# Output stores of a fused attention, Fourier-mixing and FFN kernel as a stream of steps of their own, rows of 514 elements, and a new order of the steps

## The chip, the cores and the metric

One core of one Trainium2 chip. The metric is the device time of one execution in microseconds (us), less is better. A core has five engines that work through queues of their own: TensorE (PE, with its weight loads shown as PEld), VectorE (DVE), ScalarE (ACT), GpSimd (POOL) and SyncE (SP), and DMA queues that SP, ACT and POOL issue to.

## The reference

For 8 batches of 8 heads, 576 rows and 64 columns, linear attention with a feature map, then Fourier mixing, a normalisation and an FFN:

```python
def phi(x):                                   # x: 8 x 8 x 576 x 64, w_phi: 64 x 128
    proj = np.einsum('bhsd,df->bhsf', x, w_phi)
    proj = proj - np.max(np.abs(proj), axis=-1, keepdims=True)
    return np.concatenate([np.exp(proj), np.exp(-proj)], axis=-1)
kv  = np.einsum('bhsf,bhsd->bhfd', phi(k), v)
z   = np.sum(phi(k), axis=2)
num = np.einsum('bhsf,bhfd->bhsd', phi(q), kv)
den = np.einsum('bhsf,bhf->bhs', phi(q), z)[..., None] + 1e-06
x   = (num / den)                             # heads side by side: 8 x 576 x 512
u   = x + np.real(fft(fft(x, axis=1), axis=2))
un  = (u - mean(u)) / np.sqrt(var(u) + 1e-06)
out = u + np.maximum(un @ w_ch1, 0.0) @ w_ch2 # 512 -> 2048 -> 512, fp32 out
```

## The kernel before

Every batch goes through the same stages, and stages of two or three batches run at the same time on the five engines.

**Attention.** POOL loads K, Q and V of a batch with casting DMAs (L281) into KS, QS and VS. SP turns them over by DMA transposes into KT (L411, L413) and QT (L423 to L425); for batch 0 PE does it (L371, pst) and ACT or DVE casts the result (L376, L378). PE projects K (psk, L505; batch 0: L788), ACT takes the exponentials (KPp and KPn, L511; batch 0: L794), DVE the maxima MK (L525; batch 0: L822), POOL scales V by them (V4S L444, VC L462), and PE sums kv (L844, L848). Of Q, PE makes psq (L559) for the maxima MQ (DVE, L567) and psh (L600) for the exponentials (ACT, L609). PE applies kv (pn, L969), DVE and POOL divide; POOL writes the quotient to X (L989).

**Mixing.** The rows are folded by symmetry (DVE, L862 to L886, R), multiplied by cosine and sine tables on PE (psD, L1031 and L1070; pu, L1127), and added to X (DVE, L1114). The tables SS, CS, SD and CD are made by ACT's sines at the start (L217 to L228) and doubled by DVE (L237). DVE takes the statistics (L1197), ACT writes the normalised rows UN (L1173), SP transposes them to UT (L1190).

**FFN** (`forward`, 68 steps a batch). `hidden` makes psf = W1b x UT (L1247, ACT's relu to HT L1252 or L1254) and `output(c)` makes pso (L1264) for one row block c of 128 rows; the last 64 rows are at L1290. DVE adds the scaled pso to X (L1270, L1297). Then `store(b, U, c)` issues the block's DMAs to the output, mostly on SP: four for c = 1 (L1224), one for c = 2 and c = 3 (L1230), two for c = 4 (L1233, L1234); the last half block of the last batch goes at L1320. A block of X thus holds the block of the output until it is stored, and X has three buffers.

**The order.** Nothing is scheduled by a tool at build time: every piece of work is a generator that yields between steps, and a string PLAN with one letter per step says which generator goes on next. An engine's queue is the order in which the steps issue to it; `tc.manual_schedule()` keeps it. The letters: F forward, M mixing, D folds, N normalise, U scales, P maxima of Q, T features, R maxima of K, S scaled V, K, V and Q loads, A and B the transposes of Q and K, W weight loads, G and J the first transposes on PE, C and H tables and sines, Z memsets, and Y the stirs, seven groups of four matmuls on ones whose result nobody reads (L1362). The end of `output` and the place where PLAN is read:

```python
            nc.vector.scalar_tensor_tensor(
                out=U[:, c, 0:C], in0=po[:], scalar=scale_of[b, c], in1=U[:, c, 0:C],
                op0=ALU.mult, op1=ALU.add,
            )
            store(b, U, c)
            yield
...
    with tc.manual_schedule():
        ...
        for name in PLAN:
            step(name)
```

PSUM is in three pools: pj (two buffers of two banks), pk (one) and pb (three; psf and pso among others).

Of the kernel before, what the change touches and what calls it, by code (L numbers as in the profile page):

```python
# [20 lines left out]


PLAN = (
    "CCYCCGCGZHZHCHHTZGGTHJTKHPQTTJZKRWSRJYTTRGJSSPRTYPTRJTMMYPTSTMMPSTTZPTMPTBKZTMQMMQMHTTHMMVTAMMMDYDYD"
    "TDTMRTMVTMRSMTMMMVMTRPTMTMNRMTNNTWSYMTNNMFTSPFUFMTRFMUNFFSNFFFFMNMTKNPUPPFMFMPTTTNSFPFFUUQMMMQUFFTFM"
    "FFMMFFUMFFMVFMFMFFQFBVKFKAFFTDTDTDDTFFRFFFFTFFHFFRFRFFTMTFMFRSFTFFFFFTMMFRFFSMFPTVMTFFMSTFTQNMFFFNPP"
    "MPMMMTFSMMTPFFFTSFPQTMQVMPFBFTFFNAFMMNFMFFNMFFMFMFFMFFFDFFUMFFFMFMFFTTPFFTFFTFRFDVFFTFFQFFQRKFFFDFFR"
    "FSVDTPFRKFFFMFTFTMFFMFFFVTMFFRSMFTPMFTTMNNFFMMFMQFMFFSSMTFMTFFFNFSTPPMFTFMBFPTFPAMFFFMFNTFKMMFFFNFMF"
    "MFFMFFUMQMFFVMFFFTTPFFFFMTFFRFTTFFVFFFRFFRFDFFFFDFDFFDPTFMFTTFFFFMKFRFTMSFMRFFMFTSPMFNTMPQNSFFFFQMMM"
    "MTTTFFBMSFFFFTPMTFSFFMFFMTPVMFFFFMTPNFFNNMMMFFMAFFFMUFMFKMFFFMFFTTDTTFRFFSFFFFRVFFTMFFFFFRPTFFDFFFDR"  # L30
    "FFFTDFMFVKTPFFFFFMTMBQMFFRSFMFTSTSTMMKFFFNNSFMMFMMFTFMFPTMKFFFFPTPMTFFMFFFNMFTPPMFFFTNFQMNMVFFMFQMFM"
    "FFMUFFMFFVMAFFFFTTTTFDRFRFFTFSFFFFMRFFQFFFDFFTFFFDFFRFVDFTFMFFTTMFFMFFMFRSMFQTTTMFTQFNFMSVFFMFFTNPMM"
    "FMSTPMTFFFFSMTPPMFTFFMPPFBAFMFPFMFNNFMMVFMFMFFFMTTFRMNUFFFFFMRFFFMFFFSTFFMFFPTFFTFFFDDFFFRFTFFFDFDVR"
    "FFFMFTTFFMFMTMFRFFSMFFSFMTTNTFFMFNMMFFFMMFTFMPSTFNFFFPTFMFFTMPFFFFMPSPMFFTMFFPFTMNFFFNMFMFFFUMFMFMFF"
    "FFMFFMFMFFFFFDFFDFFFFFDFFFDFMFFFMFMFFMMFFMFNFMNFFFFFFMFFFFFMNFFFMFFNFFFFFFFFFFFFFFFNUFFFFFFFFFFFFFFF"
    "FFFFFFFFFFFFFFFFFFFFFFFFFFFFFFFFFFFF"
)


# [1 line left out]
def kernel(  # L41
# [1194 lines left out]
    def forward(b):  # L1236
        U, UT = turned_u[b]
# [22 lines left out]
        def output(c):  # L1260
            at = PLACE[c]
            po = pb.tile([128, C], F32, tag="pb", name="pso")
            for hh in range(NHH):
# [6 lines left out]
            nc.vector.scalar_tensor_tensor(  # L1270
                out=U[:, c, 0:C], in0=po[:], scalar=scale_of[b, c], in1=U[:, c, 0:C],
                op0=ALU.mult, op1=ALU.add,
            )
# [156 lines left out]
```

## Time and profile before

| | us |
|---|---|
| runs | 418.07, 418.28, 424.57 |
| median | 418.28 |
| the profiled execution | 417.52 |
| its span, first to last instruction | 415.7 |

The profiled execution is one of its own, beside the three runs. 1.82 us of it lie around the span. In the profile a line such as `start us, us, engine line op out<-in xcount [idle before <-releaser]` is one instruction, or several alike in a row; the bracket is the time for which the engine stood before it, and what ended that. "SPq" and "POOLq" are the issuing of DMAs, not the transfers.

### The profile page before, as it was taken

Reading aid. Unit: us, or ns where it says so; the run is one execution under the profiler, and the core shown is the slowest. Engines: PE = TensorE matmul, PEld = TensorE weight load, DVE = VectorE, ACT = ScalarE, POOL = GpSimd, SP = SyncE. Lnnn points to the kernel's source line nnn. Section 1 sums busy time; section 2 is a strip of 40 time slices with the busy share of each in tenths; the row PEclk is TensorE's granted clock in tenths of the full one; section 3 lists DMA queues with packets and bytes.
Section 4 is the critical chain, followed back from the end, with each engine's and each line's share of the span. In section 5 each row is a group of like instructions: output and inputs, shape, how many; then the busy total and the mean of one; then the engine's idle time right before and its main releaser. Section 6 shows DMA issues by size and latency. Waiting matters only on the chain.

```text
span 415.7 us, 10465 instructions
## 1 busy us (share of the span) xinstructions
PE 391.2 (94%) x4195; PEld 265.3 (64%) x4224; DVE 317.5 (76%) x658; ACT 297.7 (72%) x548; POOL 208.1 (50%) x251
## 2 busy tenths in 40 slices
PE   4888999989999999999889999999999999999995
PEld 2556678735866568566765578566856577657564
DVE  7777887799898786898579887988889768966102
ACT  4986889778848887597858888699757886454350
POOL 4678438768746771906756382648362332301000
PEclk9899999999999999999999999999999999999998
DMA  8999798994899759663952969659882051006213
GB/s 220 195 203 146 80 187 102 135 96 88 123 161 103 96 98 152 81 99 67 139 100 40 154 118 139 91 75 101 104 125 52 18 99 33 22 7 111 36 27 88
DMA packets 108520, 42.71 MB, mean 103 GB/s; under 512 B 82615, under 2 KB 103479, under 8 KB 108471
## 3 DMA queue, kind: packets, MB, share of 16 engines
q0 software_dynamic: 46272, 16.60, 37.5%
q1 hardware_dynamic: 61703, 24.85, 33.3%
q8 instruction: 33, 0.54, 0.6%
q10 hardware_dynamic: 496, 0.59, 0.5%
q14 instruction: 16, 0.13, 0.2%
HBM read 36.77 MB, written 9.44 MB: 111 GB/s over the span
## 4 chain that ended last, share of the span: by engine, by line
PE 75%; DVE 12%; ACT 5%; POOL 3%; issue 2%; DMA 1%; POOLq 0%; DVEq 0%; ACTq 0%
PE psf L1247 27%; PE pso L1264 20%; PE pso L1290 4%; PE kv L844 4%; PE psD L1031 3%; DVE MQ L567 2%; PE pu L1127 2%; PE psk L505 2%; PE psq L559 2%; PE psh L600 1%; PE psD L1070 1%; POOL X L989 1%; DVE cb L983 1%; DVE R L862 1%; PE idle L1362 1%
## 5 line engine op out<-in xcount | busy, mean ns | idle before, releaser
L1247 PE MATMUL psf<-UT,W1b 128*128 128x320 bf16 (+1 forms) x1024 | 139.8, 286 | 1.8 <-DVE MQ L567 1.8
L1264 PE MATMUL pso<-W2b,HT 128*128 128x512 bf16 x467 | 117.2, 379 | 2.1 <-issue 1.0
L1247 PEld LDWEIGHTS <-W1b 128*128 128x128 bf16 x1024 | 95.3, 98 | 29.1 <-issue 3.8
L462 POOL TENSOR_TENSOR VC<-VS,VC 128x1024 bf16<-128x1024 bf16 x28 | 53.8, 1932 | 39.1 <-ACT VC L456 37.7
L1264 PEld LDWEIGHTS <-HT 128*128 128x128 bf16 x496 | 45.2, 98 | 43.3 <-issue 0.6
L1252 ACT ACTIVATE HT<-psf 128x320 bf16<-128x320 f32 x128 | 53.7, 437 | 25.9 <-PE psf L1247 19.0
L989 POOL TENSOR_TENSOR X<-cb,rd 128x640 f32<-128x640 f32 x28 | 35.1, 1254 | 45.9 <-DVE rd L987 25.6
L567 DVE TENSOR_REDUCE MQ<-psq 128x8 f32<-128x1024 f32 (+1 forms) x32 | 34.3, 1086 | 14.1 <-PE psq L559 13.9
L1270 DVE SCALAR_TENSOR_TENSOR X<-pso,rs,X 128x512 f32<-128x512 f32 x31 | 23.1, 744 | 28.3 <-PE pso L1264 28.1
L1254 ACT ACTIVATE HT<-psf 128x512 bf16<-128x512 f32 x64 | 37.6, 600 | 7.1 <-PE psf L1247 6.6
L525 DVE TENSOR_REDUCE MK<-psk 128x8 f32<-128x1024 f32 x28 | 33.7, 1211 | 2.9 <-ACT KPn L511 2.8
L281 POOL DMA_DIRECT2D QS<-in_q_dram x49 | 33.5, 690 | 0.9 <-issue 0.9
L609 ACT ACTIVATE QPHP<-psh 128x1024 bf16<-128x1024 f32 x28 | 28.7, 1026 | 7.2 <-PE psh L600 6.8
L511 ACT ACTIVATE KPp<-psk 128x1024 bf16<-128x1024 f32 x28 | 28.8, 1030 | 6.6 <-PE psk L505 6.3
L1173 ACT ACTIVATE UN<-X,MV 128x512 bf16<-128x512 f32 (+1 forms) x35 | 25.0, 723 | 11.8 <-DVE MV L1198 9.3
L511 ACT ACTIVATE KPn<-psk 128x1024 bf16<-128x1024 f32 x28 | 28.7, 1027 | 0.0
L609 ACT ACTIVATE QPHN<-psh 128x1024 bf16<-128x1024 f32 x28 | 28.7, 1027 | 0.0
L1197 DVE BATCH_NORM_STATS2 st<-X 128x6 f32<-128x512 f32 (+1 forms) x40 | 27.1, 678 | 0.2
L444 POOL TENSOR_TENSOR V4S<-VS,V4S 64x512 bf16<-64x512 bf16 x14 | 14.9, 1061 | 23.2 <-ACT V4S L441 21.7
L1114 DVE TENSOR_TENSOR X<-pu,X 128x512 f32<-128x512 f32 (+3 forms) x49 | 23.5, 526 | 3.7 <-PE pu L1127 3.3
L969 PEld LDWEIGHTS <-QPHP 128*128 128x128 bf16 x280 | 20.7, 98 | 7.0 <-DVE cb L983 2.8
L1213 POOL TENSOR_TENSOR rs<-VE,mhalf 128x5 f32<-128x5 f32 (+1 forms) x9 | 10.3, 1148 | 26.4 <-DVE VE L1212 26.2
(465 smaller groups left out, 771.3 us busy)
## 6 DMA issues: line engine op xcount, KB each, us to landing
out_dram<-X SPq DMA_DIRECT2D x31, 128.0 KB
out_dram<-X SPq DMA_DIRECT2D x15, 256.0 KB
KS<-in_k_dram POOLq DMA_DIRECT2D x7, 512.0 KB, 8.5
VS<-in_v_dram POOLq DMA_DIRECT2D x14, 256.0 KB, 4.9
W1b<-in_moe_w_ch_dram POOLq DMA_DIRECT2D x1, 2048.0 KB, 16.4
W2b<-in_moe_w_ch_dram POOLq DMA_DIRECT2D x1, 2048.0 KB, 16.1
QS<-in_q_dram POOLq DMA_DIRECT2D x28, 64.0 KB, 3.9
QS<-in_q_dram POOLq DMA_DIRECT2D x7, 256.0 KB, 6.0
```

The source lines that it names most:

```text
L281: nc.gpsimd.dma_start(out=pieces[i][0], in_=pieces[i][1])
L462: nc.gpsimd.tensor_tensor(out=to[:, :, :, 0:D], in0=V[:, hs, :].rearrange("p h (j d) -> p (h j) d", d=D).unsqueeze(1) .to_broadcast([128, ...
L511: nc.scalar.activation(out=KP[:, hs, :, :].rearrange("p e (jp jj) f -> p jj (e jp) f", jj=2), in_=psk[:], func=AT.Exp, scale=sgn,)
L525: nc.vector.tensor_reduce(out=MK[:, 1, 2 * pr:2 * pr + 2, :].rearrange("p e (jp jj) -> p jj (e jp)", jj=2), in_=tiles[pr][:], axis=AX.X, o ...
L567: nc.vector.tensor_reduce(out=o, in_=i[:], axis=AX.X, op=ALU.max, apply_absolute_value=True)
L609: nc.scalar.activation(out=o, in_=psh[:], func=AT.Exp, scale=sgn)
L989: nc.gpsimd.tensor_tensor(out=X[:, :, at:at + 2 * D].rearrange("p c (e d) -> p e c d", e=2), in0=cb[:, :, :, 0:D], in1=rd[:].to_broadcast( ...
L1197: nc.vector.bn_stats(out=st[0:M, :], in_=X[0:M, c, 0:C])
L1247: nc.tensor.matmul(ps, lhsT=W1b[:, cc, 128 * hh:128 * hh + 128], rhs=UT[:, cc, lo:hi], start=(cc == 0), stop=(cc == NCC - 1),)
L1252: nc.scalar.activation(out=HT[:, hh, lo:hi], in_=ps, func=AT.Relu, scale=-1.0)
L1254: nc.scalar.activation(out=HT[:, hh - 1:hh + 1, lo:hi], in_=psw[:].rearrange("p (a n) -> p a n", a=2), func=AT.Relu, scale=-1.0,)
L1264: nc.tensor.matmul(po[:], lhsT=HT[:, hh, at:at + 128], rhs=W2b[:, hh, :], start=(hh == 0), stop=(hh == NHH - 1),)
```

## The change

- `store` is no longer called from `forward`. A new generator `store_all(b)` calls it for the blocks 2, 1, 3, 4 of a batch, one a step; for the last batch 2, 1, 4, and then the two halves of block 3. It is a stream of its own, letter O, with 33 steps.
- The three places that allocate from X's pool take 514 elements a row, where they took 513. What is read and written of a row stays 512.
- PLAN is new throughout, with 1269 letters where it had 1236: the 33 O, and as many as before of every other.

```diff
 PLAN = (
-    "CCYCCGCGZHZHCHHTZGGTHJTKHPQTTJZKRWSRJYTTRGJSSPRTYPTRJTMMYPTSTMMPSTTZPTMPTBKZTMQMMQMHTTHMMVTAMMMDYDYD"
+    "CCCCCGHGHZZHZCHHYHTTGTJGRKWTQGRPTRZYSJTTJPSYRTSJTPYKRTJMMPTSTHPSMMTTPTMQPTTQVHMMMMTTMMTZMBMMYADDYDTT"
...
-        xpool.tile([128, 5, C + 1], F32, tag="X", name=n)[:].rearrange("p a b -> p (a b)")
+        xpool.tile([128, 5, C + 2], F32, tag="X", name=n)[:].rearrange("p a b -> p (a b)")
...
                 op0=ALU.mult, op1=ALU.add,
             )
-            store(b, U, c)
             yield
...
-        store(b, U, 4)
         yield
         if b < B - 1:
             return
-        rows_ = out[b, 320:576, :].rearrange("(a r j) n -> a r j n", r=32, j=2)
-        for queue, at in ((nc.scalar, 0), (nc.sync, 256)):
+        for at in (0, 256):
...
+            yield
+
+    def store_all(b):
+        U = turned_u[b][0]
+        for c in (2, 1, 3, 4) if b < B - 1 else (2, 1, 4):
+            store(b, U, c)
+            yield
+        if b < B - 1:
+            return
+        rows_ = out[b, 320:576, :].rearrange("(a r j) n -> a r j n", r=32, j=2)
+        for queue, at in ((nc.scalar, 0), (nc.sync, 256)):
             queue.dma_start(out=rows_[:, ::-1, 0, at:at + 256], in_=U[:, 3, at:at + 256])
             yield
...
-        "A": (arrive, 1), "B": (arrive_k, 1), "W": (load_ffn_weights, 2),
+        "A": (arrive, 1), "B": (arrive_k, 1), "O": (store_all, 4), "W": (load_ffn_weights, 2),
...
-    LONGER = {("N", 0): 10, ("U", 0): 7, ("M", 0): 27, ("T", 0): 20}
+    LONGER = {("N", 0): 10, ("U", 0): 7, ("M", 0): 27, ("T", 0): 20, ("O", 7): 5}
```

What the new PLAN moves shows on the engines' queues. The rows of the changed kernel carry its own line numbers: the stirs of L1362 stand at L1369 there, and L1297 at L1296.

ACT near the start, before: the casts of batch 0's turned K, the four tables, and the first exponentials of K.

```order
L383 CAST wphi_95<-wphi_f 128x128
L376 CAST KT_168<-pst 128x256
L376 CAST KT<-pst 128x512
L217 ACTIVATE SS<-gs 128x960
L221 ACTIVATE CS<-ga,halfpi 128x960
L226 ACTIVATE SD<-ga 128x512
L228 ACTIVATE CD<-ga,halfpi 128x512
L779 ACT_TABLE_LOAD
```

and with the change:

```order
L383 CAST wphi_95<-wphi_f 128x128
L376 CAST KT_168<-pst 128x256
L217 ACTIVATE SS<-gs 128x960
L376 CAST KT<-pst 128x512
L221 ACTIVATE CS<-ga,halfpi 128x960
L226 ACTIVATE SD<-ga 128x512
L228 ACTIVATE CD<-ga,halfpi 128x512
L779 ACT_TABLE_LOAD
```

The table SS has moved between the two casts. POOL at the same time, before, with the loads of batch 1 (KS and QS), the first weight load (W1b) and the scaling of batch 0's V:

```order
L281 DMA KS_271<-in_k_dram 64x8x64
L281 DMA QS_287<-in_q_dram 32x8x128 x4
L268 MEMSET V4S 128x520
L281 DMA KS<-in_k_dram 128x8x256
L91 DMA W1b<-in_moe_w_ch_dram 128x4x2048
L436 TENSOR_SCALAR MK_177<-MK_177 128x4
L444 TENSOR_TENSOR V4S<-HT,V4S 64x8x64 x2
L453 TENSOR_SCALAR MK<-MK 128x16
L462 TENSOR_TENSOR VC<-HT,VC 128x2x8x64 x2
```

and with the change:

```order
L281 DMA KS_274<-in_k_dram 64x8x64
L91 DMA W1b<-in_moe_w_ch_dram 128x4x2048
L281 DMA QS_287<-in_q_dram 32x8x128 x4
L268 MEMSET V4S 128x520
L436 TENSOR_SCALAR MK_177<-MK_177 128x4
L444 TENSOR_TENSOR V4S<-HT,V4S 64x8x64 x2
L453 TENSOR_SCALAR MK<-MK 128x16
L462 TENSOR_TENSOR VC<-HT,VC 128x2x8x64 x2
L281 DMA KS<-in_k_dram 128x8x256
```

The weight load has gone ahead of Q's four, and the large load of K behind the first pair of L462. On DVE the pair L237 stands ahead of the first casts L378, where it stood behind three of them; on PE the first stir stands behind the first eight transposes L371, where it stood ahead of them.

DVE in the fold of batch 2, where an accumulation of the FFN (L1270) and the maxima of K (L520, L525) fall between the folds, before:

```order
L879 TENSOR_TENSOR R<-R 128x2x255 x2
L883 TENSOR_TENSOR R<-R 128x2
L886 SCALAR_TENSOR_TENSOR R<-R 128x2
L520 TENSOR_REDUCE MK_1587<-ps_1602 128x4
L1270 SCALAR_TENSOR_TENSOR X<-pso,rs_1204,X 128x512
L525 TENSOR_REDUCE MK<-psk 128x2x4 x2
L1011 SCALAR_TENSOR_TENSOR R<-R,keep,pm 65x257
```

and with the change:

```order
L520 TENSOR_REDUCE MK_1596<-ps_1610 128x4
L879 TENSOR_TENSOR R<-R 128x2x255 x2
L883 TENSOR_TENSOR R<-R 128x2
L886 SCALAR_TENSOR_TENSOR R<-R 128x2
L525 TENSOR_REDUCE MK<-psk 128x2x4
L1270 SCALAR_TENSOR_TENSOR X<-pso,rs_1132,X 128x512
L1011 SCALAR_TENSOR_TENSOR R<-R,keep,pm 65x257
```

The accumulation has changed places with the first L525. On PE the third group of psk (L505) stands behind 16 matmuls of pso there, where it stood behind 26.

SP between batches 2 and 3, before: the stores of batch 2 (out), the transposes UT of batch 3 and those of batch 5's K.

```order
L1230 DMA out_dram<-X 4x32x512
L1224 DMA out_dram<-X 64x1x512 x4
L1190 DMA_TRANSPOSE UT<-UN 128x4x128 x2
L1230 DMA out_dram<-X 4x32x512
L411 DMA_TRANSPOSE KT_3510<-KS_2928 128x4x64
L413 DMA_TRANSPOSE KT<-KS 128x8x128 x2
L1233 DMA out_dram<-X 63x512
L1234 DMA out_dram<-X 1x512
```

and with the change:

```order
L1230 DMA out_dram<-X 4x32x512
L411 DMA_TRANSPOSE KT_3445<-KS_3168 128x4x64
L413 DMA_TRANSPOSE KT<-KS 128x8x128 x2
L1190 DMA_TRANSPOSE UT<-UN 128x4x128 x2
L423 DMA_TRANSPOSE QT_3628<-QS_3244 128x8x128
L424 DMA_TRANSPOSE QT_3629<-QS_3245 128x8x128
L425 DMA_TRANSPOSE QT_3630<-QS_3246 128x4x64
L1190 DMA_TRANSPOSE UT<-UN 128x4x128 x2
L1190 DMA_TRANSPOSE UT<-UN 128x4x64
L1224 DMA out_dram<-X 64x1x512 x4
L1230 DMA out_dram<-X 4x32x512
```

The stores of blocks 1, 3 and 4 stand behind all of UT and behind QT, where they stood around the first two UT. The last batch's stores stand at the end of SP's and ACT's queues in both kernels.

More of the change, by code (lines that the diff above doesn't have):

```diff
@@ L23 @@
 PLAN = (
-    "CCYCCGCGZHZHCHHTZGGTHJTKHPQTTJZKRWSRJYTTRGJSSPRTYPTRJTMMYPTSTMMPSTTZPTMPTBKZTMQMMQMHTTHMMVTAMMMDYDYD"
[L25 to L33, printed above, removed]
@@ L34 @@
-    "FFFMFTTFFMFMTMFRFFSMFFSFMTTNTFFMFNMMFFFMMFTFMPSTFNFFFPTFMFFTMPFFFFMPSPMFFTMFFPFTMNFFFNMFMFFFUMFMFMFF"
-    "FFMFFMFMFFFFFDFFDFFFFFDFFFDFMFFFMFMFFMMFFMFNFMNFFFFFFMFFFFFMNFFFMFFNFFFFFFFFFFFFFFFNUFFFFFFFFFFFFFFF"
-    "FFFFFFFFFFFFFFFFFFFFFFFFFFFFFFFFFFFF"
+    "CCCCCGHGHZZHZCHHYHTTGTJGRKWTQGRPTRZYSJTTJPSYRTSJTPYKRTJMMPTSTHPSMMTTPTMQPTTQVHMMMMTTMMTZMBMMYADDYDTT"
+    "TDMMRTSVMMRMTMKMRMTPMMTTNRVTMNTWSNTMYNNMPTFFSFTRFUUNZMFFNFSSUFMFNFFKNMMPPQTQPFMMTNTTPFUFPFUFFMMMFUTF"
+    "MUFFMFMFMFMFMFVMQBFVFKFDFFKVAFFDTTTDRTDTFFFFFHFRFFMRMFFFFTTSFFRFFTFFFTFMSFFOMRFMFQOTPMTFSFTFFFTFNMNS"
@@ new lines @@
+    "PPMMMMMTFMPMTTPFFFSFOPQTVMQMOFBTFMPNFNMMFFFMFFMFMFMFFMFAFFFNFMDFFFUFFMFFKTPTRFFDFFFFTTFTKFFVFFFFRSDO"
+    "FFRFPTFFFFFRFDVMFTTFQMFFMTFFFQMSMRFFFMTQFFTVNFMFFNFPTSFTFMTFSFNSOOVFMFMPOMMBPTMMTFFMMFFPTFFMPFANNMFM"
+    "FUTFFFMFMFFMFFMMFFMFFFTPTFFFRFMKFFKFTFRVTFTFDFFFFFFFDQFQDRFDFFTPROFFFFMQTFFFTFMMSTFFFMMRSFFTPFMTFMTB"
+    "TNNMPMFTFMFSFFFMMSTSPMMFFFTVFTPMVAMFPTFMMFFNFMFFFFNMFFFFNFMMFUFMFKOFMFOFFFMFFTTKRTTSFFFDFFTRFFFOFMFF"
+    "TFRFFFRFFTDOFFDDQFPPFFFFQMFFTTFFMMMRVQSFFFMTFTBFOMTFNFMSFFTNKFFMPTPMMMMSTPTMMFFSFFFTPMMVFTFKOMPMFOMF"
@@ new lines @@
+    "FNMMFFFFMFMFFFNFNFDMFFAFFUMFFMFFTTTTFRFFFFFTDFSFFQFFFOFRTFFRFDFFFFFRFDFVMFTFTVQMFFMFFFMTRFSMSFTVTTFM"
+    "ONTFFMFNMFSFMFMMMFTPMMFOTTPSFFFFVTPOTFQMMPFBFNNPPMFFFPMNMFFFMFMFFMFUFMFFMFAFFFMMFFFTTTTFFFFFRFDRFTFF"
+    "RDFFFFPTFFFFODFRFFFDFMFFMTTFFFMFSFVMFRMFTSFFMTOFFTNFFFMNFMTPFMSTMMFSMTTTFFFFMMFFPOTTMMFOFNNPFPSPFMPF"
+    "MMFNUFFFMFFFMMFFFMFDFFFMFFFFFMMFFFFFFFFFDFFDDFOFFFMFFFMFMFFMMFFFMFFFFNMFNMFFFFFMFFFNMFFFNFFFFFFFFFFF"
+    "FFFFFFFFFFFFNFFOUFFOFOFFFFFFFFFFFFFFFFFFFFFFFFFFFFFOFFFFFFFFOFFFOOFFO"
@@ L913, in first_heads @@
     def first_heads():
-        X = xpool.tile([128, 5, C + 1], F32, tag="X", name="X")
+        X = xpool.tile([128, 5, C + 2], F32, tag="X", name="X")
         R = fpool.tile([128, 3, 2, 512], F32, tag="R", name="R")
@@ L956, in heads @@
         E2 = made[b][5]
-        X = xpool.tile([128, 5, C + 1], F32, tag="X", name="X")
+        X = xpool.tile([128, 5, C + 2], F32, tag="X", name="X")
         R = fpool.tile([128, 3, 2, 512], F32, tag="R", name="R")
```

## The prediction

> **What bounds the kernel now.** I read the page first, its busy line, the two rows of slices for TensorE and its clock, and the shares of the chain that ended last; then a table of stretches; then the waits of TensorE.
>
> ```profile
> PE 391.2 (94%) x4195; PEld 265.3 (64%) x4224; DVE 317.5 (76%) x658; ACT 297.7 (72%) x548; POOL 208.1 (50%) x251
> PE   4888999989999999999889999999999999999995
> PEclk9899999999999999999999999999999999999998
> PE 75%; DVE 12%; ACT 5%; POOL 3%; issue 2%; DMA 1%; POOLq 0%; DVEq 0%; ACTq 0%
> ...
> 0.00:40.00 40.00, 29.50 (x379) 20.04 (x380) 30.27 (x70) 30.74 (x50) 27.48 (x54) 0.96 1.04 193
> 190.00:230.00 40.00, 36.84 (x436) 25.80 (x438) 30.30 (x63) 30.20 (x56) 27.30 (x31) 1.00 0.69 96
> 400.00:415.70 15.70, 10.71 (x93) 7.38 (x92) 2.68 (x5) 1.90 (x5) 0.00 (x0) 0.92 0.22 60
> sum 415.70, PE 391.15 PEld 265.27 DVE 317.52 ACT 297.72 POOL 208.11; mean PE 35.56 PEld 24.12 DVE 28.87 ACT 27.07 POOL 18.92
> ...
> PE psf L1247 <- DVE MQ L567: 1.8, 3, 1.3
> PE psk L505 <- DVE MK L525: 1.5, 1, 1.5
> ```
>
> TensorE is busy for 391.15 of 415.70 us, so 24.55 us is all that any new order can win. The rows (the first figure after the width is PE's busy time) say where it lies: 40.00 - 29.50 = 10.5 us before 40, 15.70 - 10.71 = 5.0 us at the tail, and so 9.05 us in the 360 us between, of which 190 to 230 alone has 3.16. The change adds no matmul and takes none away; a gain must come out of these three numbers, and the middle one must nearly vanish before anything exceeds 2%.
>
> **The start.** The change turns the order round here on four engines. These rows are ACT's, then POOL's and SP's, then two of PE, then the page's landing time of the two big loads.
>
> ```profile
> 8.73 0.37 ACT L376 CAST KT<-pst 128x256 bf16<-128x256 f32 x1 [2.81 <-PE pst L371]
> 9.77 0.59 ACT L376 CAST KT<-pst 128x512 bf16<-128x512 f32 x1 [0.67 <-PE pst L371]
> 10.25 1.01 ACT L217 ACTIVATE SS<-gs 128x960 bf16<-128x960 f32 x1
> 13.39 1.28 ACT L779 ACT_TABLE_LOAD   x1
> 17.46 1.06 ACT L794 ACTIVATE KPp<-psk 128x1024 bf16<-128x1024 f32 x1
> ...
> 14.43 0.41 DVE L237 TENSOR_TENSOR ga<-CD,flip 128x512 bf16<-128x512 bf16 x1
> ...
> 16.52 0.89 POOL L281 DMA_DIRECT2D KS<-in_k_dram  x1
> 17.40 0.76 POOL L91 DMA_DIRECT2D W1b<-in_moe_w_ch_dram  x1
> 23.43 3.82 POOL L462 TENSOR_TENSOR VC<-HT,VC 128x1024 bf16<-128x1024 f32 x2 [0.82 <-ACT VC L456]
> ...
> 22.62 9.94 SPq L413 DMA_TRANSPOSE KT<-KS  x2
> 71.49 3.02 SPq L413 DMA_TRANSPOSE KT<-KS  x2
> ...
> 42.22 0.40 PE L505 MATMUL psk<-wphi,KT 64*128 64x128 bf16 x8
> 58.62 0.61 PE L1247 MATMUL psf<-UT,W1b 128*128 128x256 bf16 x4
> ...
> KS<-in_k_dram POOLq DMA_DIRECT2D x7, 512.0 KB, 8.5
> W1b<-in_moe_w_ch_dram POOLq DMA_DIRECT2D x1, 2048.0 KB, 16.4
> ```
>
> On ACT the sine SS now stands between the two casts. Before, ACT waited 0.67 us for the second transpose and did SS afterwards; now SS starts when the first cast ends, at 9.1, and the second cast finds its transpose (pst) ready. That takes 0.67 us out of ACT, which from here to 19 us runs without another wait (the sines, the table load at 13.39, four exponentials), so the exponentials come 0.6 to 0.7 us sooner. On DVE the two L237 now precede the casts of K, and wait for ACT's cosines CD, which are done when the table load begins: 13.39 before, some 12.7 after. Two L237 of 0.41 and two casts (0.59 each by ACT's cast of that shape) end at 14.7. Their reader is the second pair of exponentials, at 17.46 and now 16.8; with 1 us for the projections between, this is covered by about 1 us. I take **-0.7**, and keep -1.5 to +1: plus if that cover is thinner than its 1 us, minus if the two waits that follow on the chain shrink as well.
>
> On POOL, W1b is issued first and the 512 KB of batch 1's K goes behind the first pair of L462, where it stands at about 27 (23.43 + 3.82) and not at 16.52. W1b then comes earlier by the issues it passes, which helps nobody: it had landed by 17.40 + 16.4 = 33.8, and its first reader is the last PE row, at 58.62. K lands at 27 + 8.5 = 35.5; the transposes took 9.94 us for two beside the W1b load and 3.02 us later, away from it, so K is turned between 38.5 and 45.5. PE wants it at 42.22. W1b would have landed by about 30 (issue near 13.7 + 16.4), before K does, so the short price is the nearer one: **0**, with 3.3 us as the bad end.
>
> **The clock at the start** moves too, since the first of the seven idle groups (four matmuls of 512 columns) no longer runs at 1.09.
>
> ```profile
> 1.09 1.89 PE L1362 MATMUL idle<-ones_b 128*128 128x512 bf16 x4 [1.09 <-DVE keep L125]
> 17.03 1.53 PE L1362 MATMUL idle<-ones_b 128*128 128x512 bf16 x4 [0.73 <-DVE MK L817]
> 21.91 1.04 PE L1362 MATMUL idle<-ones_b 128*128 128x512 bf16 x4
> 17.39:20.81 3.42, 3.07 (x19) 1.95 (x17) 2.57 (x3) 3.37 (x8) 1.76 (x4) 0.50 1.17 139
> ```
>
> The same four matmuls took 1.89, 1.53 and 1.04 us; the 17.39 to 20.81 row has a granted clock of 0.50. The group at 1.09 was followed by 5 us of idle PE, and so warmed nothing. The groups now stand between the transposes. What they can save is the excess over 1.04 at 17.03, 0.5 us, and as much again on the matmuls up to 20.8; but ACT and DVE are the chain there. I take 0, from -1 to +1 (the group put behind the first eight transposes occupies 1.89 us if it runs cold, in front of the first projection that ACT reads only at 14.68).
>
> The Trainium skill, "TensorE: Matmul & The Clock Gate", Part 1 (The HAM clock gate), has the array at half clock by default and released after a busy window of about 3.4 us on a free-running grid; by it the denser groups keep 17.39 to 20.81 at full clock, and the sum would be 1 us lower. The 0.50 in a row that is 3.42 us wide agrees with such a grid; whether the window before it counts as busy no run here shows.
>
> **The fold of batch 2, at 90 us.** First PE's row, then DVE's.
>
> ```profile
> 90.11 0.40 PE L505 MATMUL psk<-wphi,KT 64*128 64x128 bf16 x8 [1.47 <-DVE MK L525]
> ...
> 88.09 0.74 DVE L1270 SCALAR_TENSOR_TENSOR X<-pso,rs,X 128x512 f32<-128x512 f32 x1
> 88.74 2.35 DVE L525 TENSOR_REDUCE MK<-psk 128x8 f32<-128x1024 f32 x2
> ```
>
> PE stands 1.47 us until the maxima of K (L525) free the psk bank. Ahead of it on DVE is the accumulation L1270, 0.74 us, and that one now stands behind the first L525. The bank comes free 0.7 us sooner, and PE has the same matmuls behind it. Late next is the L525 itself, which waits for four folds in any case. **-0.7**, from -1.47 (the whole wait) to 0 (the accumulation now delays the free pso bank as much).
>
> **The edge between batches 2 and 3, at 200 us.** PE, SP, PE once more, ACT, DVE:
>
> ```profile
> 200.71 1.47 PE L1247 MATMUL psf<-UT,W1b 128*128 128x256 bf16 x12 [1.33 <-DVE MQ L567]
> 190.13 3.58 SPq L1224 DMA_DIRECT2D out_dram<-X  x4
> 194.00 2.78 SPq L1190 DMA_TRANSPOSE UT<-UN  x2
> 198.90 0.30 PE L844 MATMUL kv<-VC,KPp 128*128 128x65 bf16 x4
> 194.84 0.72 ACT L1173 ACTIVATE UN<-X,MV 128x512 bf16<-128x512 f32 x1
> 199.47 1.23 DVE L567 TENSOR_REDUCE MQ<-psq 128x8 f32<-128x1024 f32 x1
> ```
>
> The first hidden matmul of batch 3 waits 1.33 us. The page names the maxima of Q (they end at 200.70), but the matmul reads UT, whose two transposes are issued between 194.00 and 196.78 directly behind four stores of 512 KB in all. I read the wait as UT's landing; both endings fit the row. In the change SP has these stores behind UT, and PE has two heads of kv in the gap where it had one (ten matmuls, some 0.4 us by the kv row, which has four of them with their latency). UT's second issue was held by UN until 195.56 whatever SP did, so only the transfer, not the issue, can come sooner. **-0.5**, from -1.33 to 0; 0 if DVE's maxima are the true end.
>
> **The stores.** Taken out of the FFN they cost no compute engine anything: the row below is the largest of SP's own waits.
>
> ```profile
> SPq L1224 <- DVE X L1270: 43.1, 5, 14.8
> ```
>
> SP sat 43.1 us in five waits with nothing but a store in hand, and transposes of UT, QT and KT stood behind it. Later stores let those go first; but K, Q and UT wait also for buffers that PE frees, and of PE's waits over a microsecond only the one at 200 us is at a step that such a transpose feeds. The stores read X, of which there are three; by the place of the steps in the new order a buffer is written again more than 20 us behind its last store, and this is what hides their delay. If that cover were gone POOL's L989 would wait. **0**, from -1 to +1. At the tail the last store's place is the same: the 5.0 us stay.
>
> **The rows of 514.** Row 1 and row 3 of X begin on an odd element now, on an even one afterwards. One answer, with least, median and largest duration:
>
> ```profile
> L1197 DVE BATCH_NORM_STATS2 st<-X x40: 651/684/695, 59.9 to 381.2; 128x6 f32<-128x512 f32 x32, 64x6 f32<-64x512 f32 x8
> ```
>
> L1197 goes over each of the five rows apart, and its 40 lie within 44 ns; odd rows are no slower. **0.** POOL's writes of X and the stores' reads have no such split in the trace; I bound them by the ±1 of the stores.
>
> The Trainium skill, "Vector Engine (DVE) Microarchitecture Reference", section 5.2 (Measured stream behaviour on trn2), gives 1.30 against 1.054 ns a column for pairs that start on an odd word. By it two of five L1197 would take 0.13 us longer than the rest and the change would save that; the 651 to 695 ns disagree, and the sum by the rule would fall by less than 1 us, since DVE has idle time.
>
> **The rest of the new order.** Elsewhere the order of PE, DVE and ACT reads alike. Of the 9.05 us in the middle, 1.47 and 1.33 are used above; 6.2 remain, in pieces under 1 us that may close or open again elsewhere. **0**, from -3 to +4.
>
> Sum: -0.7 - 0.7 - 0.5 = -1.9 on the profiled execution's 417.52 us (span 415.70 and 1.82 around it): 415.6. The median shown, 418.28, lies 0.76 above that execution, so on its scale the forecast is 416.4; I say **416**.
>
> **The rivals.** *Nothing moves* (418): the three waits are not the last ones at their places, so that PE waits as long for something else. For it: SP's 43.1 us never reach PE as such. Against it: the 0.67 and 1.47 us rows name an engine whose work ahead is exactly what moves.
>
> *K of batch 1 is late* (slower): POOL's L462 hold the 512 KB load until 27, and the transposes then run at the 9.94 us pace, beside the rest of W1b or beside the loads of Q and V that POOL issues next. PE waits 3.3 us from 42.2 on (45.5 - 42.2), and loses some more if the exponentials behind it meet again at 58: 416 + 3.3 = 419.3, and 421 with half as much again. It decides as soon as the issue passes 27 + (42.2 - 38.5) = 30.7, or the transposes take over 6.7 us. Over 2% it cannot go by this alone.
>
> *The middle closes* (faster by over 2%): with stores out of SP's way every transpose lands before its reader, and the 9.05 us go, with the start's 0.7: 417.5 - 9.75 = 408. Against it: ACT and DVE are 72 and 76% busy and single waits of PE mostly name them, not a DMA.
>
> *The half-clock stretch goes* (415): with groups of idle matmuls among the transposes the row at 0.50 comes out at 1.00, the group there takes 1.04 and the other matmuls of that stretch lose a like excess, and the chain, which runs over PE's projections there, is 1 us shorter. Against it: ACT has no wait for PE in the rows of that stretch. It is the outcome that the clock gate's page of the Trainium skill would have.
>
> *The change doesn't do what it says*: a store that slips so far that L989 waits for its X. It would show as a wait of POOL for DMA; the distance of 20 us speaks against it.
>
> **How the numbers follow.** Forecast (415.5 to 417) 0.38; the half-clock stretch goes (414.5 to 415.5) 0.08; nothing moves (417 to 419) 0.21; K late, a late X or other new waits 0.18, of which 0.1 lie over 421 and 0.03 over 426; the middle closes in part or wholly 0.15, of which 0.1 lie under 411 and 0.05 under 410. Runs of this kernel can tell about 2%, 8.4 us, from no change: under 409.9 faster, over 426.6 slower. From the cases 0.05, 0.92 and 0.03. The range leaves out 0.1 at each end: 411 to 421.
>
> **What would show it.** Right: the first table load near 12.8; no wait of psk for L525 near 90, or one under 0.9; the first psf of batch 3 behind a wait under 1 us; SP's L1224 and L1230 without the long waits on L1270. Wrong: a wait before L505 near 42; PE busy share in 190 to 230 unchanged; a new wait of POOL before L989; and above all PE idle in the middle over 10 us, which would mean that the new order has opened gaps that I did not see.

## The result, and the profile after

| | runs | median, us | against before, 95% |
|---|---|---|---|
| before | 20 | 418.07 | |
| changed | 20 | 421.13 | 1.0067 (1.0040 to 1.0094) |

Medians, here and in the table of the experiments, are of all runs; the ratios leave out the runs that fell into a slower state.

The change makes the kernel slower by 0.7%. The forecast was 416, between 411 and 421: the time lies just above the range, and the sign is the wrong one. The changed kernel's profiled execution took 419.85 us (span 418.1), 2.3 more than the one before. Its runs are also spread, from 417.9 to 425.5, where most of the kernel before lie between 417.8 and 418.8; the end of this section has a part of the reason.

The page of the changed kernel, the same lines as before:

```profile
PE 390.1 (93%) x4193; PEld 263.8 (63%) x4224; DVE 317.0 (76%) x658; ACT 297.5 (71%) x548; POOL 208.6 (50%) x251
PE   2889999999987999799999999999999999999995
PEclk9999999999999999899999999999999999999999
```

PE does the same work in a longer span. In its row of slices there are two dips that were not there, an 8 and a 7 in the twelfth and thirteenth and a 7 in the seventeenth, and the clock row has an 8 at that place. The table of stretches (first figure after the width: PE busy), first two rows of before, then the changed kernel:

```profile
100.00:145.00 45.00, 44.10 (x501) 30.16 (x505) 38.89 (x78) 35.00 (x66) 30.68 (x36) 1.00 0.98 124
145.00:190.00 45.00, 44.25 (x488) 29.74 (x490) 37.80 (x77) 34.04 (x62) 21.04 (x24) 1.00 0.71 100
```

```profile
0.00:40.00 40.00, 28.46 (x385) 19.51 (x386) 31.30 (x71) 30.64 (x50) 25.71 (x50) 1.00 1.08 193
100.00:145.00 45.00, 40.63 (x480) 28.57 (x482) 36.55 (x74) 32.41 (x61) 24.57 (x30) 1.00 0.91 113
145.00:190.00 45.00, 42.21 (x464) 28.08 (x466) 34.85 (x70) 31.18 (x58) 24.98 (x28) 0.96 0.80 97
190.00:230.00 40.00, 39.65 (x447) 26.68 (x449) 32.55 (x65) 31.62 (x58) 24.67 (x27) 1.00 0.80 107
```

From 100 to 190 PE stands 4.37 + 2.79 = 7.16 us, where it stood 0.90 + 0.75 = 1.65: 5.5 us lost in two stretches for which the prediction had put down nothing. From 190 to 230 it stands 0.35 and not 3.16: 2.8 us won, at the edge that the prediction named. (Up to 40 us PE is busy 1.0 us less than before, 28.46 for 29.50, with six matmuls more in its row and a granted clock of 1.00 for 0.96.) The waits of PE say what it stood for:

```profile
PE psq L559 <- DMA QT<-QS: 3.6, 2, 2.4
PE psf L1247 <- DMA UT<-UN: 2.8, 1, 2.8
PE psk L505 <- DVE MK L525: 0.6, 2, 0.3
```

The two largest of the middle are new, and both are for a DMA transpose. One place is 173 us. PE, then SP, which issues the stores and the transposes:

```profile
173.02 0.40 PE L559 MATMUL psq<-wphi,QT 64*128 64x128 bf16 x8 [2.39 <-DMA QT<-QS]
149.77 6.05 SPq L1190 DMA_TRANSPOSE UT<-UN  x3
155.91 3.00 SPq L1224 DMA_DIRECT2D out_dram<-X  x4
160.62 3.85 SPq L411 DMA_TRANSPOSE KT<-KS  x1
172.39 1.20 SPq L425 DMA_TRANSPOSE QT<-QS  x1
```

and SP at the same place in the kernel before:

```profile
145.09 2.59 SPq L1224 DMA_DIRECT2D out_dram<-X  x4
148.52 2.54 SPq L1190 DMA_TRANSPOSE UT<-UN  x2
155.76 1.36 SPq L411 DMA_TRANSPOSE KT<-KS  x1
163.55 1.40 SPq L425 DMA_TRANSPOSE QT<-QS  x1
```

Before, the four stores of batch 1 went out at 145.09, while SP would otherwise have waited for UN. Now they stand behind three UT, right ahead of K's transposes. SP issues stores from 155.91 to 160.5, in the very time in which it turned K and Q, and K's first transpose, issued right behind them, takes 3.85 us for 1.36. Q's last transpose leaves at 172.39 and not 163.55.

The other place is 130.8. PE, SP and POOL of the changed kernel:

```profile
130.83 4.52 PE L1247 MATMUL psf<-UT,W1b 128*128 128x320 bf16 x32 [2.77 <-DMA UT<-UN]
124.63 1.18 SPq L1190 DMA_TRANSPOSE UT<-UN  x1
123.65 1.69 POOL L281 DMA_DIRECT2D KS<-in_k_dram  x2
125.33 0.76 POOL L281 DMA_DIRECT2D VS<-in_v_dram  x1
```

and of before:

```profile
128.63 1.66 PE L1247 MATMUL psf<-UT,W1b 128*128 128x320 bf16 x11
122.86 3.02 SPq L1190 DMA_TRANSPOSE UT<-UN  x2
125.84 0.85 POOL L281 DMA_DIRECT2D VS<-in_v_dram  x1
```

UT's last part is issued at about the same time in both (its issue ends at 125.8 and at 125.9), but PE gets it 2 us later. What differs is POOL: its loads begin at 123.65 and not at 125.84, and K's 576 KB are the first of them (64 and 512 KB; in the kernel before they went out at 129.90 and 137.85). They are issued ahead of that transpose, and not behind it.

**Why the runs are spread.** Behind the wait at 173 stands a second loss. Two windows of the table, cut at the edges of the clock's own record:

```profile
170.69:174.10 3.41, 0.92 (x18) 0.75 (x20) 0.64 (x1) 1.48 (x3) 0.28 (x1) 1.00 1.03 209
174.10:177.51 3.41, 3.41 (x19) 1.51 (x18) 2.16 (x4) 1.52 (x2) 0.00 (x0) 0.50 0.32 59
```

PE was busy for 0.92 of 3.41 us, and the whole next window ran at a granted clock of 0.50, which costs dense matmuls 1.7 us. The wait at 130.8, although longer, was followed by no such window: it fell across an edge (busy 1.75 and 2.31 of 3.41). The windows lie differently in every run (the first change to full clock was at 11.2 to 18.1 us in these profiles), so that a wait of 2.5 us costs 2.5 or 4.2. A stretch of 3.41 us at half clock takes 0.004 off a run's mean clock, and the twenty runs fall into groups by just that: eight at 0.992 to 0.994 with a median of 418.9 us, nine at 0.988 to 0.990 with 422.4, three at 0.986 with 424.6. The profiled execution, with its one window, has 0.994; those of experiments 1 and 2 have 0.989 and two such windows each. But the groups lie 3.5 and 2.2 us apart, and a window takes 1.7: the rest is not explained.

### The profile page after: what moved, and what is told of

It reads as the page before. It is cut to its first block, busy times and chain, and to the rows that moved or that the text cites. A ratio compares the mean times of both kernels' runs of the same rounds, so it can differ in the third digit from the quotient of the medians.

```text
span 418.1 us, 10436 instructions
## 1 busy us (share of the span) xinstructions
PE 390.1 (93%) x4193; PEld 263.8 (63%) x4224; DVE 317.0 (76%) x658; ACT 297.5 (71%) x548; POOL 208.6 (50%) x251
## 4 chain that ended last, share of the span: by engine, by line
PE 74%; DVE 15%; ACT 4%; DMA 2%; issue 2%; POOL 1%; SPq 0%; DVEq 0%; POOLq 0%; ACTq 0%
PE psf L1247 25%; PE pso L1264 22%; PE pso L1289 4%; PE kv L844 3%; PE psD L1031 2%; PE pu L1127 2%; DVE cb L983 2%; PE psh L600 2%; DVE tg L976 2%; PE psq L559 2%; DMA UT<-UN 1%; PE psk L505 1%; DVE st L1197 1%; DVE MQ L567 1%; PE psD L1070 1%
## 5 line engine op out<-in xcount | busy, mean ns | idle before, releaser
L462 POOL TENSOR_TENSOR VC<-VS,VC 128x1024 bf16<-128x1024 bf16 x28 | 53.7, 1932 | 31.9 <-ACT VC L456 31.5
L1270 DVE SCALAR_TENSOR_TENSOR X<-pso,rs,X 128x512 f32<-128x512 f32 x31 | 23.0, 743 | 34.8 <-PE pso L1264 34.8
L525 DVE TENSOR_REDUCE MK<-psk 128x8 f32<-128x1024 f32 x28 | 33.9, 1214 | 4.3 <-ACT KPn L511 3.8
L1197 DVE BATCH_NORM_STATS2 st<-X 128x6 f32<-128x512 f32 (+1 forms) x40 | 27.1, 679 | 0.4
```

Of the source, the lines that this page charges most:

```text
L462: nc.gpsimd.tensor_tensor(out=to[:, :, :, 0:D], in0=V[:, hs, :].rearrange("p h (j d) -> p (h j) d", d=D).unsqueeze(1) .to_broadcast([128, ...
L525: nc.vector.tensor_reduce(out=MK[:, 1, 2 * pr:2 * pr + 2, :].rearrange("p e (jp jj) -> p jj (e jp)", jj=2), in_=tiles[pr][:], axis=AX.X, o ...
L1197: nc.vector.bn_stats(out=st[0:M, :], in_=X[0:M, c, 0:C])
```

## The experiments

Steps are written as letter, batch and number within the batch: O1.1 is the second store step of batch 1 (the first is O1.0, block 2; then blocks 1, 3 and 4). Each ratio is taken to runs of the kernel before beside it, whose medians were 418.04 to 418.54. With intervals such as these, two ratios are clear of each other when they differ by some 0.4%, 1.6 us.

| kernel | median, us | against before, 95% |
|---|---|---|
| changed, stores of batch 1 behind the turns | 419.64 | 1.0007 (0.9982 to 1.0033) |
| changed, K load later | 421.22 | 1.0066 (1.0038 to 1.0095) |
| changed, both of these | 419.43 | 1.0028 (1.0000 to 1.0056) |
| new order, stores in the FFN | 424.10 | 1.0141 (1.0113 to 1.0169) |
| before, rows of 514 only | 417.44 | 0.9981 (0.9958 to 1.0004) |
| old order, late stores | 421.02 | 1.0071 (1.0036 to 1.0106) |
| changed, all loads behind UT | 418.13 | 0.9995 (0.9968 to 1.0021) |
| changed, stores of batch 1 at the FFN | 417.37 | 0.9976 (0.9946 to 1.0006) |
| changed, the last two together | 413.59 | 0.9890 (0.9872 to 0.9908) |
| new head, old rest | 421.52 | 1.0047 (1.0018 to 1.0077) |
| changed, stirs in the wait at 173 | 418.69 | 0.9998 (0.9964 to 1.0032) |
| the two together, rows of 513 | 413.94 | 0.9889 (0.9874 to 0.9903) |

**1. Stores behind the turns.**

```diff
-... S3.4 O1.1 O1.2 V4.1 F1.66 M2.24 F1.67 M2.25 P3.3 O1.3 M3.0 M3.1 B4.0 ... F2.6 A4.0
+... S3.4 V4.1 F1.66 M2.24 F1.67 M2.25 P3.3 M3.0 M3.1 B4.0 ... F2.6 A4.0 O1.1 O1.2 O1.3
```

> The changed kernel with one edit: the last three store steps of batch 1 (six DMAs) stand behind the transposes of K and Q (L411 to L425) on SP, where they stood ahead of them. Theory A (the postponed stores take 4.7 us of SP's queue and the DMA rings just when the transposes of K and Q are due): the 2.39 us wait of psq near 173 goes, and the half-clock stretch behind it (granted 0.55 from 174.4 to 177.8) goes too; about 3.5 us less, a median of 417.6 against the changed kernel's 421.1. Rival (Q's own load lands late, or the delay is spread over the whole order): the wait at 173 stays over 1.5 us and the time stays within 1 us of 421.

The wait at 173 is gone, and the time fell by 1.5 us in the medians and 2.5 by the ratios, not by 3.5. The delay has gone to the next transpose in the queue (PE, then SP):

```profile
180.58 1.85 PE L1247 MATMUL psf<-UT,W1b 128*128 128x320 bf16 x11 [2.42 <-DMA UT<-UN]
167.81 3.25 SPq L1224 DMA_DIRECT2D out_dram<-X  x4
172.85 4.31 SPq L1190 DMA_TRANSPOSE UT<-UN  x2
```

The stores now stand ahead of batch 2's last two UT, issued until 177.2, and PE wants those at 178.2. (The three steps are seven DMAs: four, one and two.) From 157.7 to 177.2 SP issues in this run with no pause of over 0.3 us, so there is no free slot for them in that stretch. Theory A holds as to the cause; the cure was the wrong one.

**2. The K load later.**

```diff
-F1.23 K4.0 T3.0 ... T3.4 K4.1 F1.31 F1.32 V3.1 ... F1.36 ... F1.43
+F1.23 T3.0 ... T3.4 F1.31 F1.32 V3.1 ... F1.36 K4.0 ... F1.43 K4.1
```

> The changed kernel with one edit: the two load steps of batch 4's K stand 12 FFN steps later, so that POOL issues them after 128 us and not at 123.65. Theory B (this 576 KB load fills the DMA engines while the last transpose of UT is on its way, 5 us from its issue): the 2.77 us wait of psf at 130.8 falls under 0.8 us, and the time by about 2 us, to 419. Rival (UT is late because SP issues its last part behind Q's three transposes, at 124.6): the wait stays over 2 us and the time at 421. The wait at 173 stays in both.

A miss: psf still waited 2.73 us, and the time did not move. But a load still stood ahead of UT's last transpose, V's 256 KB, which now came first; only the large K load had gone:

```profile
123.67 0.86 POOL L281 DMA_DIRECT2D VS<-in_v_dram  x1
124.53 0.72 POOL L281 DMA_DIRECT2D KS<-in_k_dram  x1
```

By the trace's semaphore updates 15 of the 16 DMA engines had finished UT's last transpose by 129.24, and one only at 130.48. So the delay does not need K's 576 KB. That any load of POOL ahead of that transpose is enough is the wider theory, which experiment 7 tried.

**3. Both moves.** The edits of 1 and 2 together.

> The changed kernel with both edits, of the stores of batch 1 and of the load of batch 4's K. If theories A and B both hold, the two losses add: 421.1 - 3.5 - 2 = 415.6, under the kernel before (418.1), with the lead of 1.65 us that the changed kernel has at the end of batch 0's FFN kept to the end. If the delay only moves to the next late transpose, 418 to 420.

419.43, 1.6 us less than the changed kernel by the ratios and no better than the first alone: neither was a cure. psf waited for UT at 130.8 (2.72) and at 179.8 (2.16).

**4. The new order with the stores in the FFN.** `store` is called from `forward` as before, and the letters O are taken out.

> The new order of all other steps and the rows of 514, with the stores issued from the FFN again as before (the letters O taken out). Theory A: the wait at 173 goes since the stores of batch 1 are out of SP's queue by 156, the wait at 130.8 stays: 418 to 418.5. Rival (the new order of the other steps is what costs): 421, with the waits at 130.8 and 173 as in the changed kernel.

424.1, slower than everything. There is no wait at 173 any more, as theory A said. But PE waited 4.12 us at 132.5, behind the same loads as in the changed kernel; why 1.3 us longer is not explained. And a wait stood at the edge between batches 2 and 3, where the four stores, and K's transposes behind them, are ahead of UT again (PE, then SP):

```profile
208.76 1.46 PE L1247 MATMUL psf<-UT,W1b 128*128 128x256 bf16 x6 [2.46 <-DMA UT<-UN]
195.96 3.13 SPq L1224 DMA_DIRECT2D out_dram<-X  x4
```

So the stream of stores as such is no loss: in the new order it is worth 3 us against stores tied to the FFN. Its places are right at the edge from 2 to 3 and wrong at that from 1 to 2.

**5. Rows of 514 alone.** `C + 1` becomes `C + 2` in the kernel before.

> The kernel before with one edit: X's rows have 514 elements. If the rows cost and gain nothing, as L1197's 651 to 695 ns over odd and even rows say: 418.1, ratio 1.000 within 0.2%. If the odd rows cost DVE 0.13 us each on the path, up to 1 us less.

417.44, with 1.000 inside the interval. Experiment 12 settles it.

**6. The old order with late stores.** The old PLAN, with each O put at the FFN step that it has in the new one.

> The kernel before with the stores as a stream of their own, at the FFN steps where the changed kernel has them, all other steps in the old order, rows of 514. Between batches 1 and 2 the stores then stand behind the first two UT but still ahead of K's transposes; between 2 and 3 they stand behind all of UT. Theory A (a store costs only where it stands ahead of a transpose that is due): the 1.33 wait at 200.7 goes, no new wait over 1 us between 120 and 180: 417 to 418. Rival (late stores cost wherever they are): a wait of over 2 us near 170 and 420 or more.

421.0, where 417 to 418 was expected. As expected, no new wait over 1 us stood between 120 and 180. But the 1.3 us wait at 201 stayed (1.52), although no store is ahead of UT there any more (PE, SP, POOL):

```profile
201.40 1.47 PE L1247 MATMUL psf<-UT,W1b 128*128 128x256 bf16 x12 [1.52 <-DMA UT<-UN]
194.48 2.77 SPq L1190 DMA_TRANSPOSE UT<-UN  x2
195.58 0.95 POOL L281 DMA_DIRECT2D QS<-in_q_dram  x1 [0.40 <-issue]
```

By the semaphore updates the first of these transposes had landed 2.4 us after its issue; the second, issued at 196.07, only at 201.26, 5.2 us after. Half a microsecond ahead of it POOL had issued 256 KB of Q. In the kernel before it is the same: that load at 195.08, the second transpose issued at 195.58 and landed at 200.58. So the stores were not what held PE there in the old order. The load looks like the cause, as at 130.8, but no run moved it.

A new wait stood at batch 6 (PE, then SP):

```profile
340.71 0.61 PE L1247 MATMUL psf<-UT,W1b 128*128 128x256 bf16 x4 [1.81 <-DMA UT<-UN]
334.80 3.34 SPq L1224 DMA_DIRECT2D out_dram<-X  x4
338.24 2.56 SPq L1190 DMA_TRANSPOSE UT<-UN  x2
```

Four stores between the first UT and the other two, which went out at 333.08 to 336.7 in the kernel before (two of the three, behind the stores): the mechanism of 173 at another place. Store places that suit one order don't suit another.

**7. All loads behind UT.**

```diff
-F1.23 K4.0 T3.0 ... T3.4 K4.1 F1.31 F1.32 V3.1 ... R3.1 S3.0 ... F1.43
+F1.23 T3.0 ... T3.4 F1.31 F1.32 ... R3.1 S3.0 V3.1 K4.0 ... F1.43 K4.1
```

> The changed kernel, with the V load and both K loads that POOL issues at 123.65 to 126.1 put behind the scaling of V (L444), so that none is issued between 110.7 and 136. Theory B' (any load of POOL issued in the 3 us ahead of UT's last transpose slows it; the run before left the V load there, and a single one of 16 engines landed at 130.48 where the others had landed by 129.24): the wait of psf at 130.8 falls under 0.8 us, the half-clock stretch that can follow goes, and the median falls by 2 to 3 us to 418.5. Rival (UT is late because of its place on SP): the wait stays over 2 us, time 421.

418.13, 3.0 us less than the changed kernel, as expected. POOL issues the loads at 134.4 and later, and PE's wait has nearly gone:

```profile
128.74 2.48 PE L1247 MATMUL psf<-UT,W1b 128*128 128x320 bf16 x17 [0.51 <-DMA UT<-UN]
```

UT's place on SP is unchanged (issued at 124.6), so the rival falls: it was the loads. By the semaphore updates 15 DMA engines had finished UT's last transpose by 127.06, and one at 128.69. The other wait is still there, and 3.52 us long in this execution.

**8. Stores of batch 1 at the FFN's steps.**

```diff
-F1.55 M2.21 ... F1.63 M2.23 ... S3.4 O1.1 O1.2 V4.1 F1.66 M2.24 F1.67 M2.25 P3.3 O1.3 M3.0
+F1.55 O1.1 M2.21 ... F1.63 O1.2 M2.23 ... S3.4 V4.1 F1.66 M2.24 F1.67 O1.3 M2.25 P3.3 M3.0
```

> The changed kernel, with the last three store steps of batch 1 moved 10, 2 and 0 FFN steps ahead, to where the FFN itself would issue them, so that the four large ones are issued before UT's wait and not behind it. Theory A: no wait of PE over 1 us between 140 and 185, neither for Q's transposes (2.39 in the changed kernel) nor for UT (2.42 when the stores stood behind them); the wait at 130.8 stays: about 418.5. Rival (KT and QT are late by the order of the other steps): the wait at 173 stays and the time at 421.

417.37, 3.8 us less than the changed kernel, with three letters moved. The four stores are issued at 147.8, while SP would otherwise wait for UN, and ahead of UT. No wait remains in that stretch:

```profile
145.00:190.00 45.00, 44.97 (x497) 29.73 (x495) 38.40 (x76) 34.51 (x65) 25.52 (x29) 1.00 0.94 110
```

**9. The last two together.**

> The changed kernel with both cures: the stores of batch 1 issued at the FFN's own steps, and POOL's V and K loads behind the scaling of V. If the two losses are separate and each is a transpose that comes late, they add: 421.1 - 3.7 - 3.0 = 414.4, with no wait of PE over 1.5 us between 100 and 260 and no stretch at half clock there. If one cure only moves the delay to the next transpose (as the stores behind the turns did): 417 to 418.

413.59 us, below 414.4, and the five runs lie within 0.7 us. It is the fastest of all, 1.1% under the kernel before. As expected, no wait of PE over 1.5 us is left between 100 and 260, and no stretch at half clock.

```profile
100.00:145.00 45.00, 43.54 (x497) 29.69 (x495) 38.31 (x76) 33.57 (x65) 27.63 (x31) 1.00 0.84 109
145.00:190.00 45.00, 44.97 (x499) 29.77 (x498) 37.88 (x76) 35.54 (x67) 25.25 (x31) 1.00 1.10 126
190.00:230.00 40.00, 39.96 (x466) 27.48 (x465) 34.14 (x70) 31.19 (x58) 26.38 (x29) 1.00 0.83 95
```

The span is 411.8 us, with PE busy for 390.4 of it, as in the changed kernel (390.1). Two late transposes account for the whole loss and hid 4.5 us that the new order had won.

**10. New head, old rest.** PLAN up to F1.23 from the changed kernel, all behind it from the kernel before, the stores of batches 1 to 7 at the FFN's steps.

> The order of the changed kernel for the first 372 steps (the start, batch 0 and the fold of batch 2, up to FFN step 24 of batch 1), the old order for all that follows, with the stores of batches 1 to 7 at the FFN's own steps. If the prediction's first two terms are right, and the loss lies wholly behind 110 us: the 1.65 us that the changed kernel leads by at the end of batch 0's FFN is kept, 416.4. Rival (the earlier head makes the same transposes late in the old order): 418 or more, with a wait of psf for UT near 128.

421.52, the rival. The 1.65 us lead at the end of batch 0's FFN is there, and then (PE, then POOL):

```profile
131.13 2.16 PE L1247 MATMUL psf<-UT,W1b 128*128 128x320 bf16 x8 [3.28 <-DMA UT<-UN]
123.64 0.86 POOL L281 DMA_DIRECT2D VS<-in_v_dram  x1
```

In the kernel before the same load, in the same old order, went out at 125.84. Leading by some 2 us, POOL puts it ahead of UT's last transpose. UT does not share the lead (issued at 124.57, for 124.60 before), since K's two transposes ahead of it on SP took 6.44 us to issue, for 4.90. The collision is a consequence of the gain at the start.

**11. Stirs in the wait at 173.**

```diff
+    def stir_there(b):
+        for i in range(2):
+            ps = pb.tile([128, 512], F32, tag="pb", name="stir")
...
-F2.21 T4.0 P4.0 T4.1
+F2.21 T4.0 X0.0 X0.1 P4.0 T4.1
```

> The changed kernel with eight matmuls on ones, 1.7 us of work whose result nobody reads, in PE's queue ahead of the psq that waits at 173. They fill most of the 2.39 us wait. If the half-clock stretch behind that wait is a consequence of the idle time (the window from 171.0 to 174.4 had PE busy for 1.23 of 3.41 us): the stretch at 174 to 178 goes and psk of batch 5 comes 1.5 us earlier, the median falls by 1 to 1.5 us to 420. Rival (the half clock has another cause): the stretch stays, and the time is 421 or more.

418.69, 2.4 us less than the changed kernel (2.9 by the ratios), with 1.9 us of useless matmuls added:

```profile
171.52 1.90 PE L1379 MATMUL stir<-ones_b 128*128 128x512 bf16 x8
173.35 0.40 PE L559 MATMUL psq<-wphi,QT 64*128 64x128 bf16 x8
```

psq starts at 173.35 with no idle time shown ahead of it, and the half-clock window behind it is gone. The profile still has one at 131.5 to 134.9, behind the wait at 130. That the gain is more than the 1.5 us allowed for is not explained; runs of such kernels spread over several us.

**12. The two together, rows of 513.**

> The kernel with both cures (413.59, its runs within 0.7 us), with X's rows of 513 elements again. The rows alone, in the old order, gave 417.44 against 418.04, too near to tell from no change. If rows of 514 are worth nothing: 413.6 within 0.3. If they are worth the 0.6 us seen there: 414.2.

413.94 against 413.59, where the runs of each lie within 0.7 us: rows of 514 are worth 0.3 us or nothing. Against the runs of the kernel before that were taken beside each, 0.9889 and 0.9890, it is nothing.

## Why the prediction was wrong

- **What bounds the kernel** was right: PE's work, and so only its idle time. But the sum looked for what the change would take out of the idle time, and bounded what it could put in by 4 us, without a place.
- **The stores, 0 (-1 to +1)**: this is the step that failed first. It rested on "of PE's waits over a microsecond only the one at 200 us is at a step that such a transpose feeds". That is a statement on the old order, in which the stores had gone before. The mechanism was in the text ("transposes of UT, QT and KT stood behind it") and was read in one direction only. Between batches 1 and 2 the change moved the stores from a slot in which SP waited (145.09) to right ahead of K's and Q's transposes, into a stretch in which SP had been issuing from 155.76 to 168.1 with no pause of over 0.3 us. Put at 0, they cost 3.8 us: so much is won by moving three steps back (experiment 8).
- **The rest of the new order, 0 (-3 to +4)**: this step failed too, in size: it held a loss of 3.0 us (experiment 7) in one place, POOL's loads beside UT's last transpose. The orders that I compared were each engine's own; that POOL's loads now precede a transpose on SP shows in none of them.
- **The start, -0.7**: the mechanism was right and the size a little small. ACT and PE, and then the end of batch 0's FFN in the changed kernel and before:

```profile
8.99 1.01 ACT L217 ACTIVATE SS<-gs 128x960 bf16<-128x960 f32 x1
12.61 1.28 ACT L779 ACT_TABLE_LOAD   x1
104.83 0.41 PE L1289 MATMUL pso<-W2b,HT 128*64 128x256 bf16 x4
```

```profile
106.48 0.74 PE L1290 MATMUL pso<-W2b,HT 128*64 128x256 bf16 x10
```

  The table load comes 0.78 us sooner (12.61 for 13.39), and PE comes to the first psk of batch 1 1.15 us sooner (41.07 for 42.22). With the fold, the lead is 1.65 us at the end of batch 0, against 1.4 forecast for the two. (The two casts on DVE were priced at ACT's 0.59 us; DVE's own had taken 0.69. It changes nothing here.) But its price was left out: what runs ahead brings its DMAs ahead (experiment 10).
- **The fold at 90, -0.7**: right. The wait of psk is 0.6 in two pieces, where it was 1.47, and the lead grows from 1.15 to 1.65 us.
- **The edge at 200, -0.5**: the place was right, the size too small, and the reason not the one that held. PE's idle time from 190 to 230 fell from 3.16 to 0.35 in the changed kernel and to 0.04 in experiment 9. That PE waited for UT and not for DVE's maxima was read rightly: in experiment 5, in the same order, the profile names UT (1.71). But the term rested on the stores ahead of UT, and experiment 6 took them away without taking the wait away. POOL's load of Q, half a microsecond ahead of UT's second transpose, was not among the rows that the prediction read. In the changed kernel POOL issues no load from 189.8 to 207.1, while UT goes out at 200.73 to 203.2. That this is what won the 2.8 us is not shown. So the gain here came by luck as far as the stores go, though experiment 4 shows that in the new order stores ahead of UT can bring a wait back (2.46).
- **K of batch 1**: 0 was right. It was issued at 25.93, turned between 33.30 and 37.2, and wanted by PE at 41.07.
- **The clock**: 0 was right. The half-clock stretch at 17.4 is not in the changed kernel's profile, but nor is it in those of experiments 5 and 6, which have the old start; that the change removed it is not shown. And it is worth nothing here: PE comes to the first psk of batch 1 at 42.22 with it (the kernel before) and at 42.23 without it (experiment 6). What was missing is that the same gate can turn a wait of 2 us or so in the middle into 1.7 us more. The row at 0.50 had been quoted for the start alone.
- **514**: 0 was right, by experiment 12. So was the reading of L1197 against the rule on odd words that the prediction took from the Trainium skill: its median is 683 ns with rows of 513 (experiment 12) and with rows of 514 (experiment 9).
- **The rivals**: slower through one late transpose was among them (K of batch 1), as a mechanism, at the wrong transpose; and the case that took place was given 0.18, of which 0.1 above 421, and so the range ended where it did, 0.13 us short. "The middle closes" had 408 and 0.1 below 411; with both cures 413.6 is what was in it.
- **The signs**: "the first table load near 12.8" (12.61), psk near 90 under 0.9 (0.34) and the first psf of batch 3 under 1 us (no wait) all came, and so did "PE idle in the middle over 10 us": 11.4 us from 40 to 400, for 9.05. The chance of new gaps had been seen; the places had not.

## What to carry to other kernels

When stores or loads are moved on an in-order queue, list for each the transfers that now stand behind it and the time at which each is due, stretch by stretch; an issue slot in which the queue waits anyway is free, and one in a busy stretch is not, wherever the data is ready. A lead won on one engine brings its DMAs forward too, so look at which transfers on other queues they then meet. And a range taken from the idle time that exists has no upper end: an order that leaves the bounding engine dense can still open new gaps.

## What the runs showed of the hardware

**The clock drops by fixed windows, and how idle one must be can be read.** In all these profiles the stretches at half clock within the run last 3.41 us and begin on a grid of that width. I cut the fourteen profiles into these windows and took each one between 40 and 400 us that ran at full clock with PE busy for less than 85%. In 12 of them PE was busy for 41% or less, and every one was followed by a window at half clock; in 37 it was busy for 44% or more, and none was. The nearest pair comes from one profile, that of experiment 3 (PE busy is the first figure after the width, the clock stands third from the end):

```profile
126.63:130.04 3.41, 1.39 (x13) 0.54 (x12) 2.22 (x4) 1.94 (x2) 0.00 (x0) 1.00 0.88 102
130.04:133.45 3.41, 2.70 (x11) 1.56 (x12) 1.84 (x5) 0.79 (x2) 0.00 (x0) 0.50 0.24 53
177.82:181.24 3.42, 1.50 (x12) 1.10 (x13) 3.42 (x8) 1.43 (x3) 3.42 (x6) 1.00 0.75 69
181.24:184.65 3.41, 3.41 (x28) 2.46 (x26) 2.91 (x7) 2.77 (x8) 2.51 (x4) 1.00 1.34 211
```

A window with 1.39 us of work was followed by half clock, one with 1.50 was not. In a stretch that is dense otherwise, a wait must then be about 2 us long within one window (59% of 3.41), and one that an edge cuts in two may be longer and cost nothing more. The Trainium skill, "TensorE: Matmul & The Clock Gate", Part 1, has the free-running window, which these runs bear out, and puts the drop after an idle window; here a window with 41% of work was idle enough.

**A load issued just ahead of a transpose delays it, on all 16 DMA engines.** UT's last transpose was issued at 124.3 to 124.6 in each of these runs, and the trace's semaphore updates say when each engine had finished it. With no load beside it 15 engines had by 127.06 and one at 128.69 (experiment 7). With 256 KB of V issued 0.7 to 0.9 us ahead of it the 15 had by 129.24 and 129.81, and the one at 130.48 and 131.08 (experiments 2 and 10). With 64 KB of K issued 1.0 us and 512 KB 0.2 us ahead, all had between 129.76 and 130.78 (the changed kernel). So 256 KB did it as surely as 576 KB. The one late engine is there without a load too. Why a load costs so much was not tried.
